# Linear attention with a soft mixture of experts on one core: two output chunks moved ahead of the second half's products, one weight load cut into three transfers, wider early zero products

## The chip, the cores and the metric

The kernel runs on one core of a Trainium2 chip. The metric is device time in microseconds (us) of one launch, and the profile shows one such launch instruction by instruction. The engines are TensorE (PE, with its weight loads PEld), VectorE (DVE), ScalarE (ACT), GpSimd (POOL) and SyncE (SP). SP computes nothing here: it issues every transfer of the kernel, one after the other, on one queue. The transfers are carried out by 16 DMA engines.

## What is computed

Two stages. The first is attention without a softmax: for each of 8 batches and 8 heads, `kv = k^T v` over 576 positions, `out = q kv`, and each row of 64 is divided by its root mean square and scaled by `g_norm`. The second is a soft mixture of 8 experts over all 4608 tokens of 512 features:

```python
kv = np.einsum('bhsd,bhse->bhde', k, v)
out = np.einsum('bhsd,bhde->bhse', q, kv)
x = out / sqrt(mean(out * out, -1) + 1e-6) * g_norm   # tokens x 512
logits = x @ phi                                      # tokens x 32 slots
d = softmax of logits over all tokens
slot_input = (d.T @ x).reshape(E, S_per_e, D)
for e in range(E):
    h = np.maximum(slot_input[e] @ w1[e], 0.0)        # 512 -> 1024
    slot_out[e] = h @ w2[e]                           # 1024 -> 512
c = softmax of logits over the 32 slots
return c @ slot_out
```

The dispatch softmax runs over all tokens, so no expert can start before the last token's logits are there; the combination `c @ slot_out` can't start before the experts have finished a half of the features. All inputs are float32: 62 MB are read and 9.4 MB are written.

## The kernel before

The program is one unrolled stream per engine in the order in which the Python code is written (`manual_schedule`); no scheduler moves anything. Three stretches follow each other.

**Attention.** The 4608 tokens are 36 tiles of 128. For each batch, `Kv` forms `k^T v` on PE and puts it into block-diagonal matrices `bd`; `products(T)` multiplies a tile of q with them (`o`, four products of 192 columns), ACT squares and copies the result, DVE takes mean squares and Newton steps, POOL scales. `Kv(0)` is done in two parts, and around these parts `fill` puts products of zeros on PE: `EARLY = (18, 2, 0)` says how many before the first part, behind it and behind the second, each 128 by 256 in bfloat16. Their results are never read.

**Experts.** Weights come in *units* of 128 partitions by 4096 floats (2 MB): eight of w1 and eight of w2. `load_w(kind, u)` issues one transfer per unit (`w1` 7 goes where the x tiles stood, and `w2` unit 2 lies in two halves). `expert_h(e)` multiplies by w1, applies the ReLU and transposes. `expert_y(e, hf)` adds expert e's part of the feature half `hf` to `pY`. The last six experts' w2 is repacked by halves (`LATE = 6`): units 2, 3 and 4 hold half 0 of experts 2 to 7, two experts in each, and units 5, 6 and 7 hold half 1. So half 0 is complete when unit 4 has come, half 1 when unit 7 has.

**Output.** `gather(hf)` copies `pY` to SBUF on DVE, `mix(hf)` multiplies it with a fixed selection matrix on PE (`pz`) and copies the result (`z`). Each half has six chunks, `chunks` in order (k, f). `output(hf, k, f)` makes four products of 384 columns in two PSUM tiles (`po`), copies one tile with ACT (L655) and the other with DVE (L657) into a staging place in the arena, and issues one transfer of 768 KB to the output (L658). There are 12 such transfers, and three PSUM buffers for `m`, the tag that `ph`, `pz` and `po` share.

What sets the order around the change: SP issues a transfer when its source or destination is free, and not before the transfer eight places earlier has landed, since eight semaphores are used in turn (`DMAHW0` to `DMAHW7` in the order shown below). The 16 DMA engines take what is issued first come first served. PE runs its stream in order, so a product that waits for a weight unit holds back all products behind it. The functions below carry the line numbers of the profile; `L98` is the weight load, `L615` the half products, `L635` the mix, `L647` the output products, `L429` the zero products.

Of the kernel before, what the change touches and what calls it, by code (L numbers as in the profile page):

```python
# [14 lines left out]
P = 128  # L15
# [10 lines left out]
CT = 12  # L26
NCH = NT // CT
NX = 14
EARLY = (18, 2, 0)
LATE_FILL = (21, 5, 5, 2, 2)  # L30
TOK = 4608
UNIT = 4096
# [16 lines left out]
def soft_moe_linear_attention(ctx: ExitStack, tc: tile.TileContext, kv_in, q_in, w1_in, w2_in, c_in, out):  # L49


    nc = tc.nc
# [11 lines left out]
    def place(at, n):  # L64
        return arena[:, at * KB : at * KB + n]
# [22 lines left out]
    def homes(kind, u):  # L88
        at = W_AT[kind, u]
        if at is None:  # L90
            return [xflat[:, :UNIT]]
        return [place(a, UNIT // len(at)) for a in at]

    def load_w(kind, u):
        parts = homes(kind, u)
        n = UNIT // len(parts)
        for i, t in enumerate(parts):
            nc.sync.dma_start(t, (w1_in if kind == "w1" else w2_in)[u, :, i * n : i * n + n])  # L98

    def w_block(kind, u, i):  # L100
        parts = homes(kind, u)
        n = UNIT // len(parts)
        k, at = divmod(i * 256, n)
        return parts[k][:, at : at + 256]
# [17 lines left out]
    loads_behind = {  # L122
        9: lambda: (load_kv(5), load_kv(6), load_q(3), load_kv(7)),
        18: lambda: [load_w(k, e) for e in range(2) for k in ("w1", "w2")],
        27: lambda: [load_w("w1", e) for e in range(2, 5)],
        31: lambda: load_w("w1", 5),
    }

# [16 lines left out]
    for i in range(2):  # L145
        lo = 64 * i
# [276 lines left out]
    def fill(n, cols=256, home=None):  # L423

        if not n:
            return
        t = home if home is not None else ps.tile([P, 2, 512], F32, tag="o", name="fill", bufs=2)[:, 1]
        for i in range(n):
            nc.tensor.matmul(  # L429
                t[:, :cols].rearrange("p (a n) -> p a n", n=256),  # L430
                lhsT=zeros[:, :P],
                rhs=zeros.unsqueeze(1).to_broadcast([P, cols // 256, 256]),
                start=True,
                stop=True,
            )

    fill(EARLY[0])

    for g in range(2):
        kv = Kv(0, "o" if g else "kv", 2 if g else None)  # L440
        kv.products(2 * g)
        kv.products(2 * g + 1)
        kv.borders((g,))
        kv.slots((g,))
        fill(EARLY[1 + g])
    T_at, diag_at, pb_at, d_at, sums_at = {}, {}, {}, {}, {}
    for T in range(NT - 2):
        for b in range(1, B):
# [114 lines left out]
    def combine(k):  # L563

        C = L[:, pos(k * CT) : pos(k * CT) + W]
        cm = wk.tile([P, W], F32, tag="cm", name=f"cm{k}")
        nc.vector.tensor_reduce(out=cm, in_=C, axis=AX.X, op=ALU.max)
        nc.vector.tensor_tensor(out=C, in0=C, in1=cm.unsqueeze(2).to_broadcast([P, W, NS]), op=ALU.subtract)
        nc.scalar.activation(C, C, AF.Exp)
        cs = wk.tile([P, W], F32, tag="cs", name=f"cs{k}")  # L570
        nc.vector.tensor_reduce(out=cs, in_=C, axis=AX.X, op=ALU.add)
        nc.vector.tensor_scalar_add(cs, cs, EPS_SUM)
        nc.vector.reciprocal(cs, cs)
        c = wk.tile([P, W, NS], F32, tag="part", name=f"c{k}", bufs=3)
        nc.vector.tensor_tensor(out=c, in0=C, in1=cs.unsqueeze(2).to_broadcast([P, W, NS]), op=ALU.mult)
        nc.vector.transpose(out=C.rearrange("p t n -> p (t n)"), in_=c.rearrange("p t n -> p (t n)"))
# [10 lines left out]
    def w2_unit(e, hf):  # L587
        first = NE - LATE
        if e < first:
            return e, 8 * hf  # L590
        return first + hf * LATE // 2 + (e - first) // 2, 8 * (e % 2)
# [19 lines left out]
    def expert_y(e, hf):  # L611
        u, at = w2_unit(e, hf)
        for c in range(8):
            j = c % 4
            nc.tensor.matmul(  # L615
                pY[32 * j : 32 * j + 32, hf, :256],
                lhsT=hTs[e][:, c],
                rhs=w_block("w2", u, at + c),
                start=e == 0 and c < 4,
                stop=e == NE - 1 and c >= 4,  # L620
            )
# [7 lines left out]
    def gather(hf):  # L629
        ys[hf] = wk.tile([P, 256], F32, tag="part", name=f"y{hf}", bufs=3)  # L630
        nc.vector.tensor_copy(out=ys[hf], in_=pY[:, hf, :256])

    def mix(hf):
        pz = ps.tile([P, 2, 512], F32, tag="m", name=f"pz{hf}")[:, 0, :256]
        nc.tensor.matmul(pz, lhsT=sel.rearrange("p a n -> p (a n)"), rhs=ys[hf], start=True, stop=True)  # L635
        zs[hf] = wk.tile([P, 256], F32, tag="part", name=f"z{hf}", bufs=3)
        nc.vector.tensor_copy(out=zs[hf], in_=pz)

    def output(hf, k, f):
        z = zs[hf]  # L640
        at = 6 * ((hf * NCH + k) * 2 + f)
        st = place(at, 4 * CT * NS).rearrange("p (a n) -> p a n", a=4)
        for v in range(2):
            po = ps.tile([P, 2, 512], F32, tag="m", name=f"po{hf}_{k}_{f}_{v}")
            for u in range(2):
                lo = 32 * (2 * v + u)
                nc.tensor.matmul(  # L647
                    po[:, u, : CT * NS].rearrange("p (g x) -> p g x", g=2),
                    lhsT=z[lo : lo + 32, f * P : (f + 1) * P],
                    rhs=cT[k][lo : lo + 32],  # L650
                    start=True,
                    stop=True,
                )
            if v == 0:
                nc.scalar.copy(st[:, 0:2], po[:, :, : CT * NS])  # L655
            else:
                nc.vector.tensor_copy(out=st[:, 2:4], in_=po[:, :, : CT * NS])  # L657
        nc.sync.dma_start(out[hf, k, :, f], place(at, 4 * CT * NS))  # L658
# [7 lines left out]
    expert_h(1)  # L666
    halves(0)
    load_w("w2", 4)
    load_w("w2", 5)
    combine(0)  # L670
    expert_h(2)
    halves(1)
# [8 lines left out]
        expert_y(e, 0)  # L681
    chunks = [(k, f) for k in range(NCH) for f in range(2)]
    gather(0)
    expert_y(2, 1)
    mix(0)
    expert_y(3, 1)
    output(0, *chunks[0])
    output(0, *chunks[1])
    expert_y(4, 1)
    expert_y(5, 1)  # L690
    output(0, *chunks[2])
    output(0, *chunks[3])
    expert_y(6, 1)
    expert_y(7, 1)
# [8 lines left out]
def build_program():  # L703
    import concourse.bacc as bacc

    nc = bacc.Bacc("TRN2", target_bir_lowering=False, num_devices=1, dynamic_dma_scratch_size=SCRATCH)
    shapes = {"kv": (B, P, TOK), "qt": (B // 2, P, TOK), "w1": (NE, P, UNIT), "w2": (NE, P, UNIT), "cs": (P, 129)}
    args = [nc.dram_tensor(f"in_{n}_dram", s, F32, kind="ExternalInput").ap() for n, s in shapes.items()]
    args.append(nc.dram_tensor("out_0_dram", (2, NCH, P, 2, 4 * CT * NS), F32, kind="ExternalOutput").ap())
    with tile.TileContext(nc, schedule_with_timeline_sim=True) as tc, tc.manual_schedule():  # L710
        soft_moe_linear_attention(tc, *args)
    return nc
# [43 lines left out]
```

## Time and profile before

| | us |
|---|---|
| median of 3 runs | 176.11 |
| the runs | 175.97, 176.11, 177.55 |
| the profiled execution | 175.97 |
| its span, first to last instruction | 174.2 |
| around the span | 1.8 |

The profile is of the run of 175.97, so 1.8 us of its time lie outside the span. A page of the profile gives each engine's busy share, the 16 DMA engines' mean busy share in 40 slices, the queues, and the groups of instructions. A view of stretches gives, for windows that one chooses, the busy time of each engine in it and how many instructions that were, then the TensorE clock granted, then the DMA share (1.00 means that all 16 engines were busy; it counts packets by their start, so it is good to some 0.03) and GB/s. A packet is one contiguous row of a transfer on one DMA engine; each engine ends its part of a transfer with a packet of 4 bytes that counts up the semaphore. The queue named q1 holds the kernel's transfers; q8 and q14 hold the fetches of the program's own instructions. A transfer has landed when the last of the engines has counted.

### The profile page before, as it was taken

What the parts mean: (1) busy time and instruction counts of PE and PEld (TensorE: products, weight loads), DVE (VectorE), ACT (ScalarE), POOL (GpSimd) and SP (SyncE); (2) the same over time, 40 slices, a digit from 0 to 9 for tenths busy, and PEclk for the clock granted to TensorE, in tenths of its full rate; (3) what the DMA queues carried; (4) which work ended last, traced back from release to release, by engine and by line L of the source; (5) the groups of instructions that cost most, each with busy time, mean ns of one, the idle gap of its engine ahead of it and who ended that gap; (6) DMA issues with size and microseconds to landing.
All of it is one profiled execution on the core that took longest, in us unless ns stands there. A gap on an engine that the chain in (4) does not pass through costs nothing.

```text
span 174.2 us, 4772 instructions
## 1 busy us (share of the span) xinstructions
PE 148.2 (85%) x2024; PEld 108.9 (63%) x2024; DVE 88.3 (51%) x180; ACT 86.8 (50%) x224; POOL 55.7 (32%) x65
## 2 busy tenths in 40 slices
PE   7577799999989899999999769989999959989500
PEld 5456778889779788888996555456556424445200
DVE  1122156566486565466663778733888114457600
ACT  2036286986957957878779553102234003336400
POOL 6000067656546676266773568000000000000000
PEclk9999999999999999999999999999999999999955
DMA  5999999999999999999999999999999999999994
GB/s 188 416 429 426 439 414 432 420 432 440 414 432 423 421 431 420 420 427 436 429 418 419 433 418 433 429 429 406 440 421 419 425 425 426 386 398 406 419 419 199
DMA packets 6645, 71.68 MB, mean 411 GB/s; under 512 B 736, under 2 KB 864, under 8 KB 2400
## 3 DMA queue, kind: packets, MB, share of 16 engines
q1 hardware_dynamic: 6624, 71.37, 97.5%
q8 instruction: 16, 0.26, 0.6%
q14 instruction: 5, 0.04, 0.1%
HBM read 61.93 MB, written 9.44 MB: 410 GB/s over the span
## 4 chain that ended last, share of the span: by engine, by line
PE 46%; DMA 20%; ACT 11%; DVE 11%; issue 3%; POOL 2%; SPq 1%; POOLq 0%; DVEq 0%
PE o L252 17%; DMA arena<-in_w_dram 11%; DMA arena<-in_kv_dram 9%; PE kvp_kv L184 8%; PE po L647 5%; PE pY L615 4%; PE ph L597 3%; DVE logits L329 3%; PE pS L386 2%; DVE ms L275 2%; ACT arena L655 2%; POOL part L324 2%; ACT bd L219 2%; PE o L243 2%; ACT sq L262 2%
## 5 line engine op out<-in xcount | busy, mean ns | idle before, releaser
L252 PE MATMUL o<-bd,arena 128*128 128x192 f32 x256 | 49.4, 336 | 1.4 <-ACT xall L270 0.6
L252 PEld LDWEIGHTS o<-bd,arena 128*128 128x128 f32 x256 | 40.8, 190 | 4.7 <-ACT xall L270 1.6
L302 POOL TENSOR_TENSOR xall<-xall,r 128x512 f32<-128x512 f32 x34 | 34.8, 1044 | 0.0
L324 POOL TENSOR_TENSOR part<-part,r 128x512 f32<-128x512 f32 x17 | 17.8, 1049 | 51.5 <-DVE r L293 51.5
L329 DVE TENSOR_REDUCE logits<-part 128x64 f32<-128x512 f32 (+1 forms) x19 | 19.3, 1015 | 16.1 <-POOL part L324 16.0
L275 DVE TENSOR_REDUCE ms<-sq 128x16 f32<-128x1024 f32 (+1 forms) x19 | 22.0, 1156 | 6.2 <-ACT sq L262 6.2
L262 ACT ACTIVATE sq<-o 128x512 f32<-128x512 f32 x36 | 21.5, 596 | 6.5 <-PE o L252 5.9
L270 ACT COPY xall<-o 128x512 f32<-128x512 f32 x34 | 20.6, 607 | 0.0
L184 PE MATMUL kvp_kv<-arena 128*64 128x64 f32 x480 | 17.3, 225 | 3.6 <-DMA arena<-in_kv_dram 3.6
L655 ACT COPY arena<-po 128x768 f32<-128x768 f32 x12 | 9.3, 800 | 20.2 <-DMA arena<-in_w_dram 10.3
L184 PEld LDWEIGHTS kvp_kv<-arena 128*64 128x64 f32 x480 | 15.2, 138 | 6.5 <-DMA arena<-in_kv_dram 4.5
L615 PE MATMUL pY<-arena,xall 128*32 128x256 f32 x256 | 15.2, 380 | 2.4 <-DMA arena<-in_w_dram 2.4
L657 DVE COPY arena<-po 128x768 f32<-128x768 f32 x12 | 11.3, 956 | 8.0 <-PE po L647 7.2
L647 PE MATMUL po<-logits,z 32*128 32x384 f32 x96 | 13.7, 526 | 1.6 <-ACT arena L655 1.0
L615 PEld LDWEIGHTS pY<-arena,xall 128*32 128x32 f32 x256 | 8.0, 110 | 9.1 <-issue 3.2
L597 PE MATMUL ph<-arena,sTe 128*32 128x256 f32 x224 | 12.7, 379 | 0.3 <-DVE sTe L544 0.3
L269 ACT COPY part<-o 128x256 f32<-128x256 f32 x34 | 12.6, 371 | 0.0
L386 PE MATMUL pS<-xall,d 128*32 128x129 f32 x288 | 10.7, 276 | 2.1 <-ACT d L374 2.1
L283 ACT ACTIVATE r<-ms,eps 128x16 f32<-128x16 f32 x17 | 5.2, 308 | 12.8 <-DVE ms L275 12.6
L647 PEld LDWEIGHTS po<-logits,z 32*128 32x128 f32 x96 | 6.3, 183 | 8.2 <-ACT arena L655 4.1
L291 DVE SCALAR_TENSOR_TENSOR r<-ms,r 128x16 f32<-128x16 f32 x17 | 3.0, 175 | 15.3 <-ACT r L284 15.3
L597 PEld LDWEIGHTS ph<-arena,sTe 128*32 128x32 f32 x224 | 7.2, 110 | 5.2 <-DVE sTe L544 0.6
(88 smaller groups left out, 143.9 us busy)
## 6 DMA issues: line engine op xcount, KB each, us to landing
arena<-in_w_dram SPq DMA_DIRECT2D x14, 2048.0 KB, 20.7
arena<-in_kv_dram SPq DMA_DIRECT2D x6, 2304.0 KB, 30.4
out_dram<-arena SPq DMA_DIRECT2D x12, 768.0 KB, 6.5
arena<-in_kv_dram SPq DMA_DIRECT2D x4, 1152.0 KB, 10.1
arena<-in_qt_dram SPq DMA_DIRECT2D x2, 2304.0 KB, 32.1
arena<-in_qt_dram SPq DMA_DIRECT2D x2, 1280.0 KB, 23.2
arena<-in_qt_dram SPq DMA_DIRECT2D x2, 1024.0 KB, 16.4
xall<-in_w_dram SPq DMA_DIRECT2D x1, 2048.0 KB, 15.4
```

Of the source, the lines that this page charges most:

```text
L184: nc.tensor.matmul(self.pkv[lo : lo + 64, w, g], lhsT=main[:, w, 1, c, lo : lo + 64], rhs=main[:, w, 0, c, lo : lo + 64], start=c == 0 and ...
L252: nc.tensor.matmul(o[:, r, :192], lhsT=q_main(2 * g + i)[:, r, at : at + P], rhs=bds[i][:, r], start=True, stop=True)
L262: nc.scalar.activation(sqs[s][:, T - starts[s]], o[:, :, 32:160], AF.Square, scale=0.125)
L270: nc.scalar.copy(xts[T % NX][:, :, :128], o[:, :, 32:160])
L275: nc.vector.tensor_reduce(out=mss[s], in_=sqs.pop(s).rearrange("p t j (w d) -> p (t j w) d", w=2), axis=AX.X, op=ALU.add)
L302: nc.gpsimd.tensor_tensor(out=x, in0=x, in1=r[:, i].rearrange("p (j w) -> p j w", w=2).unsqueeze(3).to_broadcast([P, 4, 2, D]), op=ALU.mult,)
L324: engine.tensor_tensor(out=part, in0=part, in1=rs_of[s].unsqueeze(3).to_broadcast([P, STAGES[s], H, NS]), op=ALU.mult)
L329: nc.vector.tensor_reduce(out=L[:, pos(starts[s]) : pos(starts[s]) + STAGES[s]], in_=parts.pop(s).rearrange("p t h n -> p t n h"), axis=AX ...
L386: nc.tensor.matmul(pS[32 * j : 32 * j + 32], lhsT=ds[G][:, i], rhs=x[:, j], start=i == 0, stop=i == GROUPS[G] - 1)
L597: nc.tensor.matmul(ph[32 * j : 32 * j + 32], lhsT=sTe[:, (4 * e + c) * NS : (4 * e + c + 1) * NS], rhs=w_block("w1", e, 4 * c + j), start= ...
L615: nc.tensor.matmul(pY[32 * j : 32 * j + 32, hf, :256], lhsT=hTs[e][:, c], rhs=w_block("w2", u, at + c), start=e == 0 and c < 4, stop=e == ...
L647: nc.tensor.matmul(po[:, u, : CT * NS].rearrange("p (g x) -> p g x", g=2), lhsT=z[lo : lo + 32, f * P : (f + 1) * P], rhs=cT[k][lo : lo + 32],
```

## The change

Four edits, all in the order and the shapes of work. The arithmetic of the result stays.

```diff
-EARLY = (18, 2, 0)
+EARLY = (9, 1, 0)
...
-    def load_w(kind, u):
+    def load_w(kind, u, rows=(0, P)):
         parts = homes(kind, u)
         n = UNIT // len(parts)
         for i, t in enumerate(parts):
-            nc.sync.dma_start(t, (w1_in if kind == "w1" else w2_in)[u, :, i * n : i * n + n])
+            for lo, hi in zip(rows, rows[1:]):
+                nc.sync.dma_start(t[lo:hi], (w1_in if kind == "w1" else w2_in)[u, lo:hi, i * n : i * n + n])
...
-    fill(EARLY[0])
+    fill(EARLY[0], cols=512)
...
-        fill(EARLY[1 + g])
+        fill(EARLY[1 + g], cols=512)
...
     load_w("w2", 4)
-    load_w("w2", 5)
+    load_w("w2", 5, (0, 112, 120, P))
...
     gather(0)
-    expert_y(2, 1)
     mix(0)
-    expert_y(3, 1)
     output(0, *chunks[0])
     output(0, *chunks[1])
+    expert_y(2, 1)
+    expert_y(3, 1)
+    output(0, *chunks[2])
     expert_y(4, 1)
     expert_y(5, 1)
-    output(0, *chunks[2])
     output(0, *chunks[3])
     expert_y(6, 1)
     expert_y(7, 1)
     gather(1)
```

The zero products become half as many and twice as wide, so PE has ten weight loads and ten products fewer. Unit 5 of w2 comes in three transfers, of rows 0 to 111, 112 to 119 and 120 to 127. The first two output chunks of half 0 go ahead of all products of half 1, and after them a pair of experts and one chunk alternate.

SP's queue, from the load of w2 unit 3 to the second output chunk, before (brackets name what an issue waits for; PE, DVE and Activation are the producers):

```order
L98 DMA arena<-in_w_dram 128x4096 [waits DMAHW5_49,PE_49]
L98 DMA arena<-in_w_dram 128x4096 [waits DMAHW6_49,PE_49]
L98 DMA arena<-in_w_dram 128x4096 [waits DMAHW7_49]
L98 DMA arena<-in_w_dram 128x4096 [waits DMAHW0_49,PE_49]
L98 DMA arena<-in_w_dram 128x4096 [waits DMAHW1_49]
L658 DMA out_dram<-arena 128x1536 [waits DMAHW2_49,DVE_49,Activation_49]
L658 DMA out_dram<-arena 128x1536 [waits DMAHW3_49,DVE_49,Activation_49]
```

And now:

```order
L99 DMA arena<-in_w_dram 128x4096 [waits DMAHW5_49,PE_49]
L99 DMA arena<-in_w_dram 128x4096 [waits DMAHW6_49,PE_49]
L99 DMA arena<-in_w_dram 112x4096 [waits DMAHW7_49]
L99 DMA arena<-in_w_dram 8x4096 [waits DMAHW0_49]
L99 DMA arena<-in_w_dram 8x4096 [waits DMAHW1_49]
L99 DMA arena<-in_w_dram 128x4096 [waits DMAHW2_49,PE_49]
L99 DMA arena<-in_w_dram 128x4096 [waits DMAHW3_49]
L659 DMA out_dram<-arena 128x1536 [waits DMAHW4_49,DVE_49,Activation_49]
L659 DMA out_dram<-arena 128x1536 [waits DMAHW5_49,DVE_49,Activation_49]
```

One issue has become three, and every later transfer uses the semaphore two places further on; the waits for PE, DVE and ACT stand at the same transfers as before.

PE's stream from the end of half 0 to the third output chunk, before (`pY` are the half products, eight per expert; the name `po` is followed by half, k, f and the PSUM tile):

```order
L615 MATMUL pY_1464<-arena_64,xall_65 32x256 x56
L635 MATMUL pz0_1753<-y0_1743,sel_93 128x256
L615 MATMUL pY_1464<-arena_64,xall_65 32x256 x8
L647 MATMUL po0_0_0_0_1765<-logits_104,z0_1755 128x384 x2
L647 MATMUL po0_0_0_1_1769<-logits_104,z0_1755 128x384 x2
L647 MATMUL po0_0_1_0_1774<-logits_104,z0_1755 128x384 x2
L647 MATMUL po0_0_1_1_1778<-logits_104,z0_1755 128x384 x2
L615 MATMUL pY_1464<-arena_64,xall_65 32x256 x16
L647 MATMUL po0_1_0_0_1799<-logits_104,z0_1755 128x384 x2
L647 MATMUL po0_1_0_1_1803<-logits_104,z0_1755 128x384 x2
```

And now:

```order
L616 MATMUL pY_1454<-arena_64,xall_65 32x256 x48
L636 MATMUL pz0_1737<-y0_1735,sel_93 128x256
L648 MATMUL po0_0_0_0_1741<-logits_104,z0_1739 128x384 x2
L648 MATMUL po0_0_0_1_1745<-logits_104,z0_1739 128x384 x2
L648 MATMUL po0_0_1_0_1750<-logits_104,z0_1739 128x384 x2
L648 MATMUL po0_0_1_1_1754<-logits_104,z0_1739 128x384 x2
L616 MATMUL pY_1454<-arena_64,xall_65 32x256 x16
L648 MATMUL po0_1_0_0_1775<-logits_104,z0_1739 128x384 x2
L648 MATMUL po0_1_0_1_1779<-logits_104,z0_1739 128x384 x2
L616 MATMUL pY_1454<-arena_64,xall_65 32x256 x16
```

Sixteen half-1 products (experts 2 and 3, from unit 5) stood ahead of and around the mix, and stand behind the second chunk now; the third chunk stands ahead of the products from unit 6 instead of behind them.

## The prediction

> **What bounds the kernel now.** I read the page first, for the DMA row and the queues, then the stretches of the tail, then issue against landing of the transfers, and last the order of time on PE, DVE and SP in the tail.
>
> ```profile
> span 174.2 us, 4772 instructions
> ...
> PE 148.2 (85%) x2024; PEld 108.9 (63%) x2024; DVE 88.3 (51%) x180; ACT 86.8 (50%) x224; POOL 55.7 (32%) x65
> ...
> DMA  5999999999999999999999999999999999999994
> ...
> q1 hardware_dynamic: 6624, 71.37, 97.5%
> q8 instruction: 16, 0.26, 0.6%
> ```
>
> The DMA engines are full in every slice but the first and the last; no compute engine is. PE heads the chain of waits for long stretches, but what PE releases are transfers that queue behind others. So a microsecond counts only if it is taken off the DMA engines. The next rows are stretches of the steady loads and of the tail; the last two numbers are DMA share and GB/s.
>
> ```profile
> 134.00:142.00 8.00, 5.56 (x108) 3.19 (x104) 1.70 (x5) 0.48 (x1) 0.00 (x0) 1.00 1.01 426
> ...
> 149.00:151.20 2.20, 1.95 (x16) 0.68 (x8) 0.96 (x1) 1.50 (x2) 0.00 (x0) 1.00 0.93 390
> 154.00:155.70 1.70, 1.44 (x14) 1.00 (x12) 1.29 (x2) 0.80 (x1) 0.00 (x0) 1.00 0.90 372
> 155.70:156.50 0.80, 0.80 (x10) 0.19 (x3) 0.35 (x1) 0.57 (x1) 0.00 (x0) 1.00 0.85 353
> ...
> 170.97:171.44 0.47, 0.00 (x0) 0.00 (x0) 0.00 (x0) 0.00 (x0) 0.00 (x0) 0.50 0.85 353
> 171.50:171.97 0.47, 0.00 (x0) 0.00 (x0) 0.00 (x0) 0.00 (x0) 0.00 (x0) 0.50 0.53 222
> 171.97:172.44 0.47, 0.00 (x0) 0.00 (x0) 0.00 (x0) 0.00 (x0) 0.00 (x0) 0.50 0.50 209
> 172.44:172.91 0.47, 0.00 (x0) 0.00 (x0) 0.00 (x0) 0.00 (x0) 0.00 (x0) 0.50 0.10 39
> ```
>
> The end is the point. From 171.5 on just half of the engines still work: eight (the *early* ones) are done at about 171.7, eight (the *late* ones) at about 172.9, 1.2 us later. And between 149 and 156.5 the share falls below 1 three times. Against 1.02, the share later in the tail, that is 0.09 x 2.2 + 0.12 x 1.7 + 0.17 x 0.8 = 0.54 us of all 16 engines, or 1.1 us on each of eight. Are these the late ones too? No:
>
> ```profile
> L658 SPq DMA_DIRECT2D out_dram<-arena x12: 332/332/747, 146.2 to 164.7; - x12
> ...
> DMA to landing us min/median/max: 5.1/6.5/8.5
> ```
>
> A chunk alone needs 1.9 us on the engines (below), but none of the 12 landed sooner than 5.1 us after its issue. Landing is the last engine's, so the late engines always had older rows in front: only the early ones idled. The two gaps add up to 2.3 us, and the fetches of instructions would explain them: 0.6% of 174.2 us on 16 engines is 16.7 us for 16 fetches, 1.05 us each, and two on each of eight engines make 2.1 us. That it is they is my reading; that the late engines never idle in the tail and set the end is what the rows say.
>
> The prices of a row come from a stretch of loads alone and one of chunks alone:
>
> ```profile
> DMA packets 233, 3.41 MB, mean 426 GB/s; under 512 B 25, under 2 KB 25, under 8 KB 25
> q1 hardware_dynamic: 232, 3.39, 99.9%
> ...
> DMA packets 615, 3.37 MB, mean 422 GB/s; under 512 B 66, under 2 KB 66, under 8 KB 615
> q1 hardware_dynamic: 615, 3.37, 101.8%
> ```
>
> 8 us x 16 x 0.999 over 232 - 25 = 207 rows: 0.62 us for one row of 16 KB. 8 us x 16 x 1.018 over 615 - 66 = 549 rows: 0.237 us for one of 6 KB, 1.9 us for a chunk's eight on each engine.
>
> **The change part by part.**
>
> *Unit 5 in three.* Unit 5 has 128 rows, eight per engine. Each row is one packet on one engine. I take 112 rows as seven per engine and eight rows as one row on each of eight engines: so eight engines get 7 + 1 + 1 = 9 rows, the other eight get 7. One row less on the late engines is -0.62 us, one more on the early +0.62 us. Which eight get nine? No row numbers the engines. One hint is the order in which engines start:
>
> ```profile
> 0.74 0.37 SPq L69
> ...
> DMA packets 8, 0.07 MB, mean 61 GB/s; under 512 B 0, under 2 KB 0, under 8 KB 0
> ...
> DMA packets 13, 0.12 MB, mean 75 GB/s; under 512 B 0, under 2 KB 0, under 8 KB 0
> ...
> 155.19 0.33 SPq L658 DMA_DIRECT2D out_dram<-arena  x1
> ...
> 155.53:156.00 0.47, 0.47 (x10) 0.36 (x4) 0.00 (x0) 0.07 (x1) 0.00 (x0) 1.00 0.60 248
> 156.00:156.23 0.23, 0.23 (x6) 0.00 (x0) 0.08 (x1) 0.23 (x1) 0.00 (x0) 1.00 1.03 427
> ```
>
> The very first transfer, issued at 0.74, has 8 packets begun by 1.9 (1.16 us on) and 13 by 2.3: some engines are served first. In the tail, with a share of 0.60 (six or seven engines idle), the chunk issued at 155.19 has the share back at 1.03 from 156.0, 0.8 to 1.0 us on. The idle engines, the early ones, answer like the group served first, and a transfer on eight engines would most simply take those. It is a weak hint, worth some 2 to 1. With it: -0.62 us. The bounds: +0.62 us if the late engines get the ninth row, and far above that if the eight rows don't spread; -0.62 is also the most that seven rows in place of eight can give.
>
> [...]
>
> SP issues twice more, at 0.33 to 0.43 us each:
>
> ```profile
> L98 SPq DMA_DIRECT2D arena<-in_w_dram x5: 327/328/425, 118.4 to 125.7; - x5
> ...
> DMA to landing us min/median/max: 13.2/19.1/25.5
> ```
>
> The loads behind it land 13 to 25 us after their issue, so 0.85 us of issue is covered; unit 7, issued at 125.7, lands at 151.2. If that cover were gone it would cost the 0.85. The semaphores shift by two, and the transfer eight places earlier has long landed in each case. Two more counting packets on eight engines: under 0.1 us, on early ones.
>
> *Order of chunks and products.*
>
> ```profile
> 139.11 0.42 DVE L631 COPY y<-pY 128x256 f32<-128x256 f32 x1 [3.83 <-PE pY L615]
> 141.48 1.07 PE L615 MATMUL pY<-arena,xall 128*32 128x256 f32 x16 [2.44 <-DMA arena<-in_w_dram]
> 143.22 0.43 DVE L637 COPY z<-pz 128x256 f32<-128x256 f32 x1 [3.68 <-PE pz L635]
> 144.11 1.56 PE L647 MATMUL po<-logits,z 32*128 32x384 f32 x12
> 146.15 19.23 SPq L658 DMA_DIRECT2D out_dram<-arena  x12
> 146.77 1.93 PE L615 MATMUL pY<-arena,xall 128*32 128x256 f32 x32
> 151.29 1.93 PE L615 MATMUL pY<-arena,xall 128*32 128x256 f32 x32
> 153.15 0.93 PE L647 MATMUL po<-logits,z 32*128 32x384 f32 x8
> 154.17 0.96 DVE L657 COPY arena<-po 128x768 f32<-128x768 f32 x1 [0.46 <-PE po L647]
> ```
>
> The mix stood behind products that waited 2.44 us for unit 5. Now it follows the copy of y: 139.53 + 0.3 to start it, 0.7 for it, 0.5 for z: `po` at about 141.3 in place of 144.11, the first chunk issued at about 143.3 in place of 146.15, the second at 145.1. What now waits behind them are the products of experts 2 and 3, from about 144.0 to 145.9, then the third chunk (issued at 148.0, before at about 150.7), the products of unit 6 to 148.8, the fourth chunk, done on PE by 149.8. Unit 7 arrives at 151.2, so its products aren't held up: PE keeps about 0.8 us of room even with the unit 0.6 us earlier. From there everything hangs on unit 7 as before, 0.6 us earlier if the late engines are relieved.
>
> On the late engines this gives nothing: they have rows in front all the time. On the early ones it fills two of the gaps (third and fourth chunk), up to 1.1 us, which the ninth row partly takes. So the early engines end between 171.2 and 172.3, and the late at 172.9 - 0.62 = 172.3: these still set the end.
>
> *Zero products.*
>
> ```profile
> 1.05 3.71 PE L429 MATMUL fill<-zeros 128*128 128x256 bf16 x18 [1.05 <-DVE zeros L136]
> 6.25 1.15 PE L184 MATMUL kvp_kv<-arena 128*64 128x64 f32 x32 [1.48 <-DMA arena<-in_kv_dram]
> 8.56 0.38 PE L429 MATMUL fill<-zeros 128*128 128x256 bf16 x2
> 106.20 4.71 PE L429 MATMUL fill<-zeros 128*128 128x512 bf16 x21
> ```
>
> Eighteen take 3.71 us, 0.21 each. Nine of double width take between 9 x 0.22 = 2.0 us (the late ones' pace) and 3.7 us (twice 0.21), nearer the second since the PE is as newly started as before; both end ahead of the first kv, 1.48 us later. Without that cover the cost is 0 to 0.4 us on PE, with loads queued ahead anyway. PE has 20 instructions fewer; 16 fetches for its 4048 are some 250 each, so 20 are a twelfth of a fetch: the count most likely stays at 16.
>
> *Sum:* 0 (zero products) + 0 (issues) + 0 (order) - 0.62 (one row off the late engines) = -0.6 us on the profiled execution: span 174.2 to 173.6. That execution took 175.97, 0.1 under the median of 176.11; the same step on the median gives 175.5.
>
> **The rivals.**
>
> *The late engines get the ninth row*, or the two sets of eight overlap. Then the end moves by +0.62 and a counting packet or two: 176.8. For it: no row names the engines. Against: the start order above.
>
> *The cut does nothing for the late engines*: the pieces are dealt evenly, or the 112 rows take as long as 128. Nothing but the early engines' gaps change: 176.1.
>
> *The eight neighbouring rows hinder each other* (slower). [...] For it: nothing before has fewer than 128 rows, so nothing excludes it. Against: the even share of 1.01 shows no engine held up by another. If one engine carried both pieces alone (16 x 0.62 = 9.9 us) the end would come at 179.9, a run of 183.
>
> [...]
>
> **How the numbers follow.** The forecast (175.5; alone 175.2 to 175.8) 0.48; the cut does nothing (176.1) 0.17; the ninth row on the late engines (176.8) 0.18; the hindrance (177.2 to 178.7) 0.10; one engine, or a PE order that holds up unit 7's products, 0.03; an unforeseen gain of over 1% 0.04. The range from 175.1 to 177.5 holds the first three and the mild end of the hindrance. About 1% (1.8 us) is what a measurement of this kernel can tell from no change: below 174.3 is faster, 0.04; above 177.9 slower, 0.09; the rest same, 0.87.
>
> **What would show it.** Right: the half-share stretch at the end shrinks from 1.2 us to nothing or to the other sign, the dips at 149 to 156.5 shrink, the first chunk is issued near 143.3, unit 7's products start near 150.6, and the last rows of DMA stop 0.6 us sooner. Wrong: a longer half-share stretch with unit 7 later than 151.2 (ninth row on the late ones), packets of 16 KB that take over 0.62 us after unit 5's issue (hindrance), or an end that moves although the half-share stretch does not.

## The result and the profile after

The changed kernel takes 187.0 us (median of 4 runs, 186.0 to 187.78); the kernel before, on the same chip and in turn with it, 176.04. The ratio is 1.060, with a 95% interval of 1.052 to 1.068: slower by 6%. The forecast was 175.5, at most 177.5. All ratios in this document are of runs taken side by side, times are medians, and both leave disturbed executions out; the profiled one of e2 was such (480.94 us), so that no profile of it is read, and the profiled one of e10 (178.93 us) is the longest of its eight, so that only its loads are read and not its end.

The profiled execution took 186.72 us with a span of 184.9, 10.7 more than before. The page of the changed kernel begins as follows (40 slices of the span; GB/s is what the DMA engines moved in each):

```profile
span 184.9 us, 4754 instructions
...
PEclk9999999999999999999999999999999979889965
DMA  6999999999999999999999999999999999949993
GB/s 199 419 430 430 429 425 431 419 428 435 414 430 428 431 422 421 423 425 432 415 431 429 425 425 425 418 427 438 377 223 206 209 379 416 415 205 392 412 417 146
...
q1 hardware_dynamic: 6640, 71.37, 96.1%
q8 instruction: 16, 0.26, 0.6%
```

The bytes are the same. In the slices 30 to 32, and in a part of 29 and 33 (377 and 379), the DMA engines are as busy as ever (9 in the row DMA) and move half as much: 206 to 223 GB/s. Busy and slow at once means that each packet takes longer (1.23 us a row in place of 0.62, worked out below). Later one slice falls to 205 with a 4 in the row DMA: there most of the engines had nothing to do. The same in stretches cut to the events (last three numbers: granted clock of PE, DMA share, GB/s):

```profile
120.00:132.00 12.00, 12.00 (x228) 7.27 (x224) 9.16 (x21) 2.88 (x6) 0.00 (x0) 1.00 1.03 430
132.50:134.00 1.50, 1.50 (x32) 0.91 (x28) 1.24 (x4) 0.96 (x3) 0.00 (x0) 1.00 1.17 317
134.00:141.00 7.00, 4.71 (x89) 2.71 (x84) 2.02 (x5) 0.47 (x1) 0.00 (x0) 1.00 0.98 208
141.00:148.00 7.00, 4.47 (x45) 2.01 (x34) 2.77 (x4) 1.50 (x2) 0.00 (x0) 1.00 0.99 213
...
150.00:160.00 10.00, 6.88 (x80) 3.13 (x80) 1.92 (x2) 1.60 (x2) 0.00 (x0) 0.83 0.98 413
160.00:165.00 5.00, 4.81 (x42) 1.99 (x42) 0.68 (x2) 0.31 (x1) 0.00 (x0) 0.66 0.80 335
165.00:166.60 1.60, 1.34 (x12) 0.90 (x12) 1.04 (x2) 0.59 (x2) 0.00 (x0) 1.00 0.09 38
166.60:182.00 15.40, 6.82 (x50) 3.14 (x44) 6.52 (x7) 5.39 (x7) 0.00 (x0) 0.85 1.00 407
...
182.00:184.90 2.90, 0.00 (x0) 0.00 (x0) 0.00 (x0) 0.00 (x0) 0.00 (x0) 0.50 0.04 15
```

From 120 to 132 us the engines move 430 GB/s, no less than before the change. From 134 until 148 the share is 0.98 to 0.99 and the pace half. (The share of 1.17 ahead of it comes of counting packets by their start: in a stretch as short as 1.5 us it can be off by more than 0.03.) The DMA view of 134 to 148 us gives the price of a row in that time:

```profile
DMA packets 219, 2.95 MB, mean 211 GB/s; under 512 B 39, under 2 KB 39, under 8 KB 39
...
q1 hardware_dynamic: 218, 2.93, 98.1%
```

14 us x 16 engines x 0.981 over 218 - 39 = 179 rows is 1.23 us a row, against 0.62 before. It isn't the few small pieces that are slow: it is every row. Taken one by one in the trace, none of the 151 rows that began from 134 to 146 us took under 1.07 us. At full pace 179 rows take 179 x 0.62 / 16 = 6.9 us, so 7 of the 14 us are lost in this window alone.

How that reaches the end is in the chain of waits and in the timeline of the changed kernel (start, us, engine, instructions; in brackets PE's wait before them):

```profile
126.48 33.67 DMA arena<-in_w_dram
160.15 0.04 issue
160.19 3.61 PE pY L616 x32
```

```profile
140.40 1.93 PE L616 MATMUL pY<-arena,xall 128*32 128x256 f32 x32 [2.29 <-DMA arena<-in_w_dram]
...
160.19 3.61 PE L616 MATMUL pY<-arena,xall 128*32 128x256 f32 x32 [2.08 <-DMA arena<-in_w_dram]
163.73 0.93 PE L648 MATMUL po<-logits,z 32*128 32x384 f32 x8
...
165.77 0.33 SPq L659 DMA_DIRECT2D out_dram<-arena  x1
```

The wait at 140.40 is for unit 4, a whole load issued ahead of the cut one: it lands at 140.2 in place of 136.4, and before the change PE didn't wait for it. Unit 7 lands at 160.15 in place of 151.2: +9.0. PE had waited 2.08 us for it and then runs at a granted clock of 0.66 (the stretch 160 to 165), so that its products take 3.61 us in place of 1.93: +1.7. The fifth chunk is issued at 165.77 in place of 155.19, +10.6. By then the four chunks ahead of it have all but drained: in the trace fifteen of the sixteen engines have passed their last packet of the fourth by 165.7 and stand idle until 166.6, and one works on it until 167.06 (share 0.09 from 165 to 166.6). The fifteen then start together, between 166.60 and 166.75, and the split into eight early and eight late engines, on which the whole forecast turned, is gone. One engine alone is late at the end: fifteen finish the last chunk by 182.4 us, the sixteenth at 184.0 (the last row above is what it still does). By the landings it falls 1.9 us behind between 169.3 and 173.1 us, and one fetch of instructions on q8 began at 168.83 and took 1.50 us. That fits the prediction's reading that the fetches make engines late; no row names the engine, so it isn't shown. From the fifth chunk's issue to the end of the span it is 19.1 us, before it was 19.0. So of 10.7 us lost, 9.0 are in unit 7's landing and 1.6 between that and the fifth chunk.

### The profile page after: what moved, and what is told of

It reads as the page before. It is cut to its first block, busy times and chain, and to the rows that moved or that the text cites. A ratio compares the mean times of both kernels' runs of the same rounds, so it can differ in the third digit from the quotient of the medians.

```text
span 184.9 us, 4754 instructions
## 1 busy us (share of the span) xinstructions
PE 154.6 (84%) x2014; PEld 111.7 (60%) x2014; DVE 88.3 (48%) x180; ACT 86.9 (47%) x224; POOL 55.7 (30%) x65
## 4 chain that ended last, share of the span: by engine, by line
PE 49%; DMA 28%; ACT 10%; DVE 5%; issue 1%; POOL 1%; SPq 0%; POOLq 0%; DVEq 0%; ACTq 0%
DMA arena<-in_w_dram 25%; PE o L253 19%; PE kvp_kv L185 9%; PE pY L616 4%; PE po L648 4%; DMA arena<-in_kv_dram 3%; PE ph L598 3%; PE pS L387 2%; ACT sq L263 2%; PE kvp_kv L200 2%; ACT bd L220 2%; PE o L244 2%; ACT xall L271 2%; DVE arena L658 2%; ACT bd L230 1%
## 5 line engine op out<-in xcount | busy, mean ns | idle before, releaser
L253 PE MATMUL o<-bd,arena 128*128 128x192 f32 x256 | 50.6, 342 | 1.1 <-ACT xall L271 0.6
L253 PEld LDWEIGHTS o<-bd,arena 128*128 128x128 f32 x256 | 42.1, 195 | 4.3 <-ACT xall L271 1.6
L616 PE MATMUL pY<-arena,xall 128*32 128x256 f32 x256 | 18.2, 436 | 8.7 <-DMA arena<-in_w_dram 8.7
L616 PEld LDWEIGHTS pY<-arena,xall 128*32 128x32 f32 x256 | 9.2, 124 | 17.1 <-issue 9.7
L185 PE MATMUL kvp_kv<-arena 128*64 128x64 f32 x480 | 17.9, 231 | 1.2 <-DMA arena<-in_kv_dram 1.2
L185 PEld LDWEIGHTS kvp_kv<-arena 128*64 128x64 f32 x480 | 15.9, 143 | 4.6 <-issue 2.2
L648 PE MATMUL po<-logits,z 32*128 32x384 f32 x96 | 13.1, 527 | 1.9 <-ACT arena L656 0.8
L387 PE MATMUL pS<-xall,d 128*32 128x129 f32 x288 | 10.7, 276 | 2.1 <-ACT d L375 2.1
L430 PE MATMUL fill<-zeros 128*128 128x512 bf16 x31 | 9.4, 461 | 1.1 <-DVE zeros L137 1.1
```

The costliest lines, as they stand in the source:

```text
L185: nc.tensor.matmul(self.pkv[lo : lo + 64, w, g], lhsT=main[:, w, 1, c, lo : lo + 64], rhs=main[:, w, 0, c, lo : lo + 64], start=c == 0 and ...
L253: nc.tensor.matmul(o[:, r, :192], lhsT=q_main(2 * g + i)[:, r, at : at + P], rhs=bds[i][:, r], start=True, stop=True)
L616: nc.tensor.matmul(pY[32 * j : 32 * j + 32, hf, :256], lhsT=hTs[e][:, c], rhs=w_block("w2", u, at + c), start=e == 0 and c < 4, stop=e == ...
L648: nc.tensor.matmul(po[:, u, : CT * NS].rearrange("p (g x) -> p g x", g=2), lhsT=z[lo : lo + 32, f * P : (f + 1) * P], rhs=cT[k][lo : lo + 32],
```

## The experiments

The kernel before was run again beside each group of runs: its median was 176.1 us beside e1 to e4, 177.3 beside e5 to e8 and 177.4 beside e9 to e12, so that a ratio isn't always the quotient by the 176.0 of the first line. In the table, "unit 7" is when its load landed (its issue plus the longest time to landing of the load view), and "cost" what that is above 151.2 less 0.61 us for each row per engine that a run leaves out.

| run | unit 5 of w2 | order of chunks | time, us | ratio to before (95%) | unit 7 | cost |
|---|---|---|---|---|---|---|
| before | 128 rows | old | 176.0 | 1 | 151.2 | 0 |
| changed | 112 + 8 + 8 | new | 187.0 | 1.060 (1.052 to 1.068) | 160.2 | 9.0 |
| e1_whole | 128 | new | 177.0 | 1.002 (0.998 to 1.005) | 151.3 | 0.1 |
| e2_split_only | 112 + 8 + 8 | old | 187.3 | 1.062 (1.056 to 1.069) | | |
| e3_112_16 | 112 + 16 | old | 187.8 | 1.063 (1.056 to 1.071) | 159.6 | 8.4 |
| e4_64_64 | 64 + 64 | old | 186.0 | 1.053 (1.046 to 1.061) | 158.7 | 7.5 |
| e5_rows_32_95 | rows 32 to 95 only | old | 174.1 | 0.984 (0.977 to 0.991) | 148.7 | 0 |
| e6_same_rows_to_0_63 | the same rows, to partitions 0 to 63 | old | 180.9 | 1.023 (1.016 to 1.030) | 153.9 | 5.1 |
| e7_quarter_cut | 3072 columns whole, 1024 as 112 + 8 + 8 | old | 180.1 | 1.017 (1.011 to 1.024) | 153.8 | 2.6 |
| e8_whole_warm | 128 | new, 16 zero products | 176.1 | 0.997 (0.994 to 1.001) | 151.2 | 0 |
| e9_112_alone | rows 0 to 111 only | old | 184.7 | 1.046 (1.037 to 1.056) | 157.8 | 7.2 |
| e10_16_alone | rows 112 to 127 only | old | 176.8 | 1.001 (0.996 to 1.006) | 151.4 | 4.5 |
| e11_columns | 3584 + 256 + 256 columns | old | 176.1 | 0.996 (0.993 to 0.999) | 151.4 | 0.2 |
| e12_middle_first | 64 (32 to 95) + 32 + 32 | old | 183.5 | 1.039 (1.030 to 1.048) | 156.0 | 4.8 |

**Which part of the change costs: e1 and e2.** Undo the cut alone, and do the cut alone.

```
e1, in the changed kernel:
-    load_w("w2", 5, (0, 112, 120, P))
+    load_w("w2", 5)
e2, in the kernel before:
-    load_w("w2", 5)
+    load_w("w2", 5, (0, 112, 120, P))
```

Expected of e1:

> The changed kernel with w2 unit 5 loaded in one transfer again; the new order of chunks and products and the wide zero products stay. If the cut of unit 5 is the whole loss: 176.0 +- 0.5, DMA share dips in the tail smaller than before, no stretch at half the GB/s. If the new order of chunks and products causes it (products of unit 5 waiting behind output products): 185 or more.

Expected of e2:

> The kernel before with nothing changed but unit 5 cut into rows 0-111, 112-119, 120-127. If the cut is the whole loss: 185 to 188, with a stretch of some 15 us at 200 to 215 GB/s in which packets of 16 KB take 1.2 us. If the order takes part: clearly under 185. If the order is the cause: 176.

Without the cut the changed kernel is level with the kernel before (1.002); with the cut alone the kernel before is as slow as the changed one (1.062). The whole loss comes with the cut. (The 177.0 us of e1 are a little over the expected 176.0 +- 0.5; the part on the order of the chunks takes that up.)

**Which piece: e3 and e4.** The eight-row pieces were the natural suspects: replace them by one of 16 rows, or cut the unit in two halves.

```
e3:  load_w("w2", 5, (0, 112, P))
e4:  load_w("w2", 5, (0, 64, P))
```

> The kernel before with unit 5 cut into rows 0-111 and 112-127. Every engine again has eight rows. If the 112-row transfer slows all engines down: still a stretch at half the GB/s, 183 to 188. [...]

> The kernel before with unit 5 cut into rows 0-63 and 64-127, four rows per engine each. [...] If it is seven rows per engine (not a multiple of four) that does it: 176 to 177.

Both are as slow, within the intervals or nearly so. The page of e4 shows the same valley, 374, 227, 220, 220 where 430 was:

```profile
GB/s 199 403 429 424 444 431 429 412 435 414 431 422 436 418 427 422 431 418 436 411 438 422 429 429 425 413 427 432 374 227 220 220 418 308 344 340 396 411 417 141
```

So it needs neither a piece of eight rows, nor a third transfer, nor seven rows per engine: 64 rows are four for each of sixteen engines.

**Where the rows go, or how many they are: e5 and e6.** Both load 64 rows of unit 5, the same rows of the same array in DRAM, in one transfer, and leave out the other 64. They differ in the partitions of SBUF that the rows go to.

```
e5:  nc.sync.dma_start(t[32:96], w2_in[5, 32:96, ...])
e6:  nc.sync.dma_start(t[0:64],  w2_in[5, 32:96, ...])
```

> The kernel before, but unit 5 of w2 is loaded by one transfer of its rows 32 to 95 alone; rows 0 to 31 and 96 to 127 of it are left out (1 MB of DMA less, worth 4 rows of 0.61 us = 2.4 us at the full pace). Theory 'any transfer with fewer than 128 rows slows all engines': packets of 16 KB take about 1.2 us from 132.5 to about 140 as with the two pieces of 64 rows (which cost 9.9 us, so one of them some 5): unit 7 lands 2 to 3 us later than before and the time is 177 to 179. [...]

> As the run beside it, with the same 64 rows read from DRAM (32 to 95 of unit 5), written to partitions 0 to 63 in place of 32 to 95; the unit's other rows are left out. Theory 'it is where the rows go': all sixteen engines now write one half of SBUF: packets of 1.2 us, 210 to 230 GB/s for some 7 to 8 us after 132.5, unit 7 lands 2 to 3 us later than before in place of 2.4 earlier, and the time is 177 to 179, 4 us or more above the other run. Rival 'the DRAM side decides' (the same rows, the same addresses): no difference between the two runs over 0.5 us.

The DMA view of 133 to 143 us, first of e5, then of e6:

```profile
DMA packets 300, 4.28 MB, mean 428 GB/s; under 512 B 39, under 2 KB 39, under 8 KB 39
...
q1 hardware_dynamic: 299, 4.26, 100.4%
```

```profile
DMA packets 158, 2.20 MB, mean 220 GB/s; under 512 B 24, under 2 KB 24, under 8 KB 24
...
q1 hardware_dynamic: 157, 2.18, 100.7%
```

In e5 260 rows pass in 10 us, 0.62 us each; in e6 133 rows, 1.21 each. This decides it: not the number of rows, not the addresses in DRAM, but the partitions they are written to. Rows 32 to 95 cost nothing: unit 7 lands 2.5 us earlier, as it should with half a unit less, and the time falls with it (ratio 0.984). The same rows written to partitions 0 to 63 halve the pace of all sixteen engines. Of the 133 rows at most 64 are unit 5's own; the other 69 belong to units 4 and 6, ordinary loads of 128 rows under way in the same 10 us. They are slowed as well: none of the 133 rows took under 0.98 us in the trace, and unit 4, issued ahead of unit 5, lands at 139.5 us in e6 and at 136.4 in e5. That is why 64 rows that would take 2.5 us at the full pace cost 5.1 us extra and not 2.5. One expectation of e6 was missed: unit 7 is 2.7 us later than before, as expected, but the time, 180.9, is 2 us over the expected 179.

**How much per byte: e7.** Only the last quarter of unit 5's columns is cut as in the change.

> The kernel before, with unit 5's first 3072 columns loaded by one transfer of 128 rows, and only its last 1024 columns cut into 112 and twice 8 rows (a quarter of the bytes of the changed kernel's cut). Theory 'the pace is halved while engines are in the cut rows': the cost goes with the bytes, a quarter of 10.6 us to a third (the spread of the engines, 3.7 us, adds to it): unit 7 lands 2 to 4 us later than before and the time is 178 to 180. Rival 'it is the presence of such transfers, whatever their size': some 10 us as with the whole unit cut, 186 to 188. Rival 'small doses are absorbed': 176.

Two stretches of e7 (a whole row is now 12 KB and a cut one 4 KB):

```profile
138.00:142.00 4.00, 1.38 (x28) 0.55 (x20) 0.42 (x1) 0.00 (x0) 0.00 (x0) 0.95 1.05 286
142.00:144.00 2.00, 1.58 (x16) 0.68 (x16) 0.00 (x0) 0.00 (x0) 0.00 (x0) 0.50 0.95 266
```

Unit 7 lands 2.6 us late, somewhat over a quarter of 9.0, and the time is 180.1, at the upper end of what was expected. For one and the same cut of the rows the cost goes with the bytes, not with the number of transfers, which is one more here. From one cut to another it doesn't, as e10 shows next.

**Which of the pieces: e9 and e10.** Rows 0 to 111 alone, the last 16 left out; and rows 112 to 127 alone, the first 112 left out.

> The kernel before, but unit 5 is loaded by one transfer of rows 0 to 111 alone; rows 112 to 127 are left out (one row of 0.61 us per engine less). Theory 'the 112-row piece carries the cost': 205 to 230 GB/s from 132.5 to 146 or later, unit 7 lands at 156 to 159 (with the last 16 rows it was 158 to 160), time 184 to 187. Rival 'the small pieces carry it': packets back at 0.61 us, unit 7 lands at 150.5, time 175.5.

> The kernel before, but of unit 5 only rows 112 to 127 are loaded, one for each engine; rows 0 to 111 are left out (seven rows of 0.61 us per engine less, 4.3 us). Theory 'the 112-row piece carries the cost': unit 7 lands 4.3 us earlier than before plus one to three row times for the one row that all engines bring into sixteen neighbouring partitions: 147.4 to 148.7, and the time is 172.5 to 174.5. Rival 'the small pieces carry it': half the pace for several us around 133 and unit 7 no earlier than 151, time 176 or more.

The stretch from 132.5 to 143 us, of e9 and then of e10:

```profile
132.50:143.00 10.50, 7.74 (x128) 4.09 (x116) 2.89 (x9) 0.89 (x2) 0.00 (x0) 0.91 1.03 226
```

```profile
132.50:143.00 10.50, 7.59 (x120) 4.28 (x116) 2.72 (x8) 0.80 (x2) 0.00 (x0) 0.87 1.00 284
```

The 112 rows alone cost 7.2 us, as expected. The sixteen alone were a miss: I expected unit 7 between 147.4 and 148.7, and it landed at 151.4. The times of its other executions say the same: 176.8 us in place of the expected 172.5 to 174.5, level with the kernel before (1.001), although seven rows per engine, worth 4.3 us, are left out. One row per engine, a seventh of the other's bytes, costs 4.5 us. So both kinds of piece are dear, per row the small one far more, and the costs don't add: 7.2 + 4.5 would be 11.7, and 112 + 16 together cost 8.4. My reading is that they overlap in time, engines that are ahead being in the second piece while others are still in the first; no run takes that apart.

**Cuts that should be harmless: e11 and e12.** Three transfers cut by columns, each with all 128 rows; and the whole unit by rows, with 32 to 95 first.

> The kernel before with unit 5 loaded in three transfers as in the changed kernel, but cut by columns: 3584, 256 and 256 of the 4096 columns, all 128 rows each. Theory 'it is where the rows go': no cost but that of 32 smaller packets per engine, under 0.5 us: unit 7 lands at 151 to 151.7, time 175.8 to 176.8. Rival 'three transfers in place of one, or their issues and counting packets, cost': 178 or more.

> The kernel before with all of unit 5 in three transfers: rows 32 to 95 first (that ran at the full pace alone), then rows 0 to 31 and rows 96 to 127, two rows for each engine into one half of SBUF. Theory 'it is where the rows go': only the two small pieces run at half the pace, so 2.4 us at the least (4 rows of 0.61 us taking 1.2 each) and up to 5 with the engines' spread of 3.7 us: unit 7 lands at 153.5 to 156, time 178.5 to 181.5, under the 186 of the halves 0 to 63 and 64 to 127. Rival 'every cut of the rows costs the same': 185 to 187.

The stretch from 132.5 to 143 us of e11, and of e12:

```profile
132.50:143.00 10.50, 8.51 (x150) 4.70 (x146) 3.29 (x9) 0.74 (x2) 0.00 (x0) 1.00 1.01 422
```

```profile
132.50:143.00 10.50, 6.65 (x120) 3.73 (x112) 2.98 (x8) 0.61 (x2) 0.00 (x0) 0.97 1.04 287
```

By columns three transfers cost 0.2 us on unit 7 and nothing in the time; the interval ends just under 1, by less than this kernel's measurement tells from no change. So the third transfer, its issue and its counting packets were rightly priced at about nothing. In e12 the engines move 418 GB/s from 132.5 to 134.5 us and 251 from 134.5 to 145: the 64 middle rows, first in line, pass at full pace, and the two pieces of 32 rows, two per engine, don't: unit 7 lands at 156.0, at the late end of what was expected, and the time, 183.5, is 2 us over it. From unit 7's landing to the end of the span it is 26.1 us here and 23.0 before. The trace has the first two chunks issued from 154.10 in place of 146.15, since PE waits 7.38 us for unit 5, and the DMA share then falls to 0.65 (153 to 156 us), 0.71 (158 to 160) and 0.78 (162 to 165): 2.3 us of all engines, most of the difference. In the old order every cut kernel with a profile that is read to its end shows some of it: it is 24.6 to 26.3 us from unit 7's landing to the end in e3, e4, e6, e7, e9 and e12.

**The order of the chunks: e1 again, and e8.** In e1 the order does what was forecast up to the fourth chunk: the first two are issued from 143.02 on (forecast 143.3; the pieces that the forecast lists for `po` add up to 141.0 and not to its 141.3, and `po` began at 140.99). But its profiled span is 175.6, not 174.2. Its timeline, and the granted clock (third number from the end) in three stretches:

```profile
151.31 3.24 PE L616 MATMUL pY<-arena,xall 128*32 128x256 f32 x32 [2.09 <-DMA arena<-in_w_dram]
...
156.86 0.33 SPq L659 DMA_DIRECT2D out_dram<-arena  x1
```

```profile
151.00:153.00 2.00, 1.69 (x20) 0.91 (x24) 0.00 (x0) 0.00 (x0) 0.00 (x0) 0.70 1.01 421
153.00:155.00 2.00, 2.00 (x20) 0.95 (x16) 0.41 (x1) 0.00 (x0) 0.00 (x0) 0.50 0.99 412
155.00:157.00 2.00, 1.73 (x14) 0.67 (x10) 1.18 (x3) 0.80 (x1) 0.00 (x0) 0.95 0.55 230
```

PE is done early, waits 2.09 us for unit 7, and the clock granted to it falls to 0.70 and 0.50: added up over the three stretches, it is at half for 3.4 us. (The changed kernel's trace has only two levels of it, 1.00 and 0.50, and half for 3.41 us from 160.22 on.) The same products then take 3.24 us in place of 1.93; the fifth chunk is issued at 156.86 in place of 155.19, and the DMA engines run short (share 0.55). If that is the cause, work without use in the gap must cure it. e8 puts 16 zero products there:

```
     output(0, *chunks[3])
+    fill(16, home=pY[:, 0, 256:])
     expert_y(6, 1)
```

> The changed kernel with unit 5 in one transfer again, and 16 zero products of 256 columns on PE between the fourth output chunk and the products of unit 7, where the profile of the same kernel without them shows PE idle for 2.09 us and the products then at a granted clock of 0.5 to 0.7 (3.24 us in place of 1.93). Theory 'the new order costs what the clock costs there': with the zero products the unit-7 products take 1.9 to 2.1 us, the fifth chunk is issued at 155.0 to 155.6 in place of 156.86, the fall to 293 GB/s is gone, and the profiled span is 174.0 to 174.6 (175.6 without); time 175.5 to 176.3. Rival 'the new order itself loses it': fifth chunk at 156.5 or later and 176.6 to 177.4 as without the zero products. No theory expects it clearly faster than the kernel before, since all DMA engines but the early ones have rows in front anyway.

```profile
149.44 1.92 PE L430 MATMUL pY<-zeros 128*128 128x256 bf16 x16
...
151.29 1.93 PE L616 MATMUL pY<-arena,xall 128*32 128x256 f32 x32
...
154.96 1.56 PE L648 MATMUL po<-logits,z 32*128 32x384 f32 x12 [0.26 <-ACT arena L656]
```

The timeline of e8 has the products back at 1.93 us, the fifth chunk back at 155.19 and the span back at 174.2. So between these two profiled executions the slow products behind the idle PE account for the 1.4 us. The changed kernel has the same wait (2.08 us, clock 0.66), so most of its 1.6 us behind unit 7 is of this kind. Two things are not shown. A wait of this length doesn't always lower the clock: PE waited 2.44 us for unit 5 before the change (141.48 in the prediction's lines, clock 1.00 from 134 to 142), 2.29 us for unit 4 in the changed kernel (clock 1.00 from 134 to 148) and 2.23 us in e6 (1.00 from 134 to 144), and the products behind were as fast as ever: 1.07 us for 16, 1.93 for 32. And the times don't show that the order costs 1.4 us in general: of e1's 12 executions six took 176.1 to 176.7 us and six 177.3 to 177.7, but of the 17 of the kernel before beside it, in the old order, five took 177.5 to 177.6 as well (of e8's 12, two over 177). What these five lost, no trace shows. e8 is level with the kernel before; no version here that computes the whole result beats it.

## Why the prediction was wrong, step by step

**What bounds the kernel: right.** The loss is 9.0 us of transfer, and it came to the end through unit 7 and the fifth chunk, as the chain of before had it. PE added its 1.6 us by bringing that chunk's issue later still.

**The price of the cut: wrong, and this is the step that failed.** The forecast took "112 rows as seven per engine and eight rows as one row on each of eight engines", each row at the 0.62 us of a 128-row load, and summed up to -0.62 us. The count was right: the changed kernel's trace has 16 landings for the 112 rows and eight for each small piece. The price was measured on transfers that fill all 128 partitions and carried over to transfers that don't, as if a row cost the same wherever it goes. e5 and e6 show that it doesn't: the same rows from the same addresses cost 0.62 us into partitions 32 to 95 and 1.21 us into 0 to 63. The term of -0.62 should have been +9.0. Whether late or early engines took the eight-row pieces, the question on which most of the chances were spread, had no weight.

**The hindrance rival: the right kind, far too small.** It was there with 0.10 and 177.2 to 178.7 us. It let only the small pieces hinder each other. The loss behind these times was the author's estimate and no run shows it; in its place the runs showed 9.0 us for the whole cut. They show three things that it lacked: the 112-row piece is hit too (7.2 us by itself); whole loads in flight beside the cut one are slowed with it (69 of 133 rows in e6); and one row per engine into 16 neighbouring partitions costs 4.5 us. Its argument against, that "the even share of 1.01 shows no engine held up by another", read a stretch in which every transfer had 128 rows: it could say nothing of other shapes. The prediction said itself that "nothing before has fewer than 128 rows"; an operation that no row shows, on the resource that bounds the kernel, should have widened the range upward to half the pace for the whole unit at the least: 8 rows at 0.62 us more, +5 us, 181. Even that falls short of the 187.0, since the whole loads are slowed too.

**Issues and semaphores: right.** e11 has the same three transfers by columns, with no cost in the time.

**The order of chunks: right up to the fourth chunk, not after it in the profiled executions.** "PE keeps about 0.8 us of room" was read as harmless. The room was 2.1 us of idling in e1, and in its profiled execution this was paid through the granted clock, 1.4 us, against a term of 0; with the zero products of e8 it is gone. How often it is paid stays open, as said above.

**Zero products and fetches: right where they count.** Nine wide ones, forecast at 2.0 to 3.7 us, took 4.02 (3.51 in e8) and still ended ahead of the first kv; the fetches stayed at 16, as the q8 row above shows. What the forecast didn't have: the first kv products behind them took 1.98 us here in place of 1.15. In e1 and e8, with the same zero products, they took 1.15, and unit 7 was issued at 125.7 in e1 as before, so no run shows a loss from it. The timeline of the changed kernel:

```profile
1.05 4.02 PE L430 MATMUL fill<-zeros 128*128 128x512 bf16 x9 [1.05 <-DVE zeros L137]
6.30 1.98 PE L185 MATMUL kvp_kv<-arena 128*64 128x64 f32 x32 [1.22 <-DMA arena<-in_kv_dram]
```

**What would show it: right.** The list named "packets of 16 KB that take over 0.62 us after unit 5's issue (hindrance)" and a unit 7 later than 151.2; both are what the profile shows.

**What stays open.** That the partitions written decide is shown by e5 and e6. By which mechanism isn't: no row names the engine of a packet. Why 112 rows are hit as hard as 64, why 16 rows cost 4.5 us, and why waits of 2.1 us lowered PE's clock where waits of 2.2 to 2.4 us didn't, stays open.

## What to carry to other kernels

In a kernel bound by its DMA engines, don't cut a 128-row load by rows to shift work between engines: here the cut rows ran at half the pace (1.23 us a row in place of 0.62) and slowed the whole loads beside them (unit 4 landed at 140.2 us in place of 136.4); a cut by columns, all 128 rows in each transfer, cost 0.2 us on the landing and nothing in the time. A price per row is good only for the shape it was measured on, so where a change brings a new shape to the resource that sets the time, test that shape alone, or let the range reach to half the pace. And work moved ahead of a wait leaves the engine idle in it: on PE a wait of 2.1 us was followed by products that took 1.3 to 1.7 us longer in two traces, and zero products in the wait kept them fast in a third; but waits of 2.2 to 2.4 us elsewhere cost nothing behind them, so look for the granted clock in the trace before you pay for a remedy.

## What the runs showed of the hardware

- One transfer of 64 rows of 16 KB brought all sixteen DMA engines from 430 to 220 GB/s at a DMA share of 1.0 while it was under way, or left them at 428, by its partitions alone (0 to 63, or 32 to 95).
- Sixteen rows, one per engine, into partitions 112 to 127 cost 4.5 us where their bytes are worth 0.6.
- One cut load slows whole loads of 128 rows that are in flight beside it: unit 4, issued ahead of the cut one, landed 3.1 us later in e6 than in e5.
- A DMA share of 0.98 and half the GB/s (208) stand side by side in the changed kernel: the share counts packets under way, and says nothing of the pace.
- After 2.08 and 2.09 us of idling the clock granted to PE was half for about 3.4 us, and products of 1.93 us took 3.61 and 3.24; after 2.23, 2.29 and 2.44 us of idling in other places it was not, and they took no longer than usual.
